# Unit 5 of every eight transposed by DMA instead of TensorE in a two-problem attention kernel

## The chip, the cores and the metric

The kernel runs on one core of one Trainium2 chip. The metric is the device time of one execution in microseconds, median of several runs.

## The reference

Two independent problems A and B of the same shape, outputs side by side. B repeats its keys `Hq // Hkv` = 1 times, so it is the same computation as A.

```python
B, Sq, D = 16, 144, 448
H, Sk, Dh = 16, 512, 256
q = (x @ wq).reshape(B, Sq, H, Dh).transpose(0, 2, 1, 3)
scores = einsum("bhqd,bhkd->bhqk", q, k_cache) * Dh ** -0.5
p = softmax(scores, axis=-1)
o = einsum("bhqk,bhkd->bhqd", p, v_cache)
out = o.transpose(0, 2, 1, 3).reshape(B, Sq, H * Dh) @ wo      # all bf16
```

## The kernel before

**Units.** A unit is one (problem, batch, head): 512 units in all (`NT`), 256 of A and then 256 of B. Eight units are a super-group (`SG`, 64 of them), four are a group (`G`). A unit has 144 query rows. 128 partitions don't hold them, so they are cut into `QA` = 112 rows, handled unit by unit, and a remainder of `QB` = 32 rows; the remainders of four units are stacked to one tile of 128 rows.

**Stages of a unit.**
- Q (`t_q`, L338): eight matmuls, x and Wq into one PSUM bank, moved to one of `NQT` = 12 slots of `qt_sb` by DVE or ACT (`t_evac_q`).
- SB (`t_sb`, L374): scores of the remainders of eight units at once, 16 matmuls at the first slot of a super-group; it is the first reader of the super-group's K. SA (`t_sa`, L471): scores of the 112 rows of one unit, two matmuls.
- Softmax of the 112 rows: maximum on DVE (L482), exponential with row sum on ACT into `pa_sb` (L493, `NPA` = 14 slots), reciprocal on DVE (L503), normalisation on POOL (`t_norm`, L511). The remainders do the same per group into `pb_sb` (L387, L397, L407, L415).
- P has its queries on partitions and must be transposed. The 112 rows: four TensorE transposes into PSUM (`t_ta`, L524) and a DVE copy into `pt_sb` (`t_evac_pta`, L534). The remainders: in the super-groups of `TB_SG` (0 to 7 and 28 to 37) TensorE (`t_tb`, L437) and DVE (L447); in the other 46 one transposing DMA per super-group, SBUF to SBUF, for both groups (`t_ptb_dma`, L425), from `pb_sb` into `pbt_sb`, which has one buffer (`NPBT` = 1). From `pbt_sb` POOL copies a group's remainders into `pt_sb` (`t_copy_ptb`, L457).
- PV (`t_pv`, L557): eight matmuls, moved to `ring` by ACT (L572, L574). OP (`t_op_piece`, L595): the output projection in pieces of two matmuls, spread over the slots; the result goes through `ost_sb` (`NOST` = 3 slots, L613) to the store (L624).

**Order.** The program is written out slot by slot; slot i is where unit i has its PV. In steady state SA and Q run ahead: SB of super-group n stands in slot 8n - 14, SA of unit u some 14 slots before its PV, TA (`LT`) two slots before it. Every engine executes its own list in order. `_Sched` adds the semaphore waits from the versions that each operation reads and writes; a write to a buffer waits for all readers of what it held.

**DMAs.** All are issued by SP, in one queue. `dma_plan` sorts them by a planned slot, and SP works the list off as fast as its waits let it; the planned slot sets the order only. K (`t_load_k`, L306) is 2 MB for a super-group, transposing, into one of `NK` = 2 buffers, so K of super-group n waits for the last SA of super-group n - 2. V (`t_load_v`, L316) is 1 MB for a group, five buffers. x (`t_load_x`, L296 and L297, transposing) serves two batches, 32 units. Wq (`t_load_wq`, L275 and L277) and Wo (L285) are loaded once for each problem, Wq in four quarters; B's replace A's around unit 256.

For each pair of super-groups n, n + 1 (n even, t = 8n) the list has this order (an x load stands first where (t + 32) is a multiple of 32):

```python
plan_x(t - 4, XG)
plan_pb(t - 4, n)          # the remainder's transposing DMA
plan_k(t - 3, n + 2)
plan_pb(t + 2, n + 1)
plan_k(t + 2, n + 3)
plan_v(t + 5 ...)          # three at t + 5, one at t + 8
```

and the quarters of B's Wq at `(4.9, 4.9, 8, 11)[hg] + NU - 32`, that is slots 228.9, 228.9, 232 and 235. The remainder's copies on POOL stand in slots 8n - 1 (first group) and 8n + 1 (second group).

Of the kernel before, what the change touches and what calls it, by code (L numbers as in the profile page):

```python
# [122 lines left out]
def bass_concat_heads__mha_block_cached__gqa_block_cached__near_ridge_kernel(  # L123
# [41 lines left out]
    TB_SG = set(range(RAMP)) | set(range(NSG // 2 - 4, NSG // 2 + 6))  # L165
    NK, NV, NXG = 2, 5, 2
# [5 lines left out]
    NQT, NPA, NPB, NPT, NST, NSTB, NOST = 12, 14, 2, 8, 4, 2, 3  # L172
# [9 lines left out]
    with contextlib.ExitStack() as es:  # L182
# [14 lines left out]
        pb_sb = sb("pb_sb", [128, NPB, 2, SK], BF16)  # L197
        pt_sb = sb("pt_sb", [128, NPT, 4, SQ], BF16)
        pbt_sb = sb("pbt_sb", [128, NPBT, 2, 4, 128], BF16)
# [38 lines left out]
        def t_ident():  # L238
            ones = pa_sb[:, 0, 0:128]

            def e1(g):
                return g.memset(ones, 1.0)
            S.add(POOL, e1, writes=[(("pa", 0), "ones")], name="ones")

            def e2(g):
                return g.affine_select(ident[:], ones, pattern=[[1, 128]], compare_op=ALU.is_equal,
                                       fill=0.0, base=0, channel_multiplier=-1)
            S.add(POOL, e2, reads=[(("pa", 0), "ones")], writes=[("ident", 0)], name="ident")

# [170 lines left out]
        def t_ptb_dma(SG):  # L420
            psl = SG % NPB
            tsl = SG % NPBT

            def e(q):
                return q.dma_start_transpose(pbt_sb[:, tsl, :, :, :].rearrange("p g c q -> p (g c) q"),  # L425
                                             pb_sb[:, psl, :, :].rearrange("p g k -> p (g k)")).then_inc(
                    sems["pb%d" % tsl], 16)
            S.add(SP, e, reads=[(("pb", psl, g), (2 * SG + g, 1)) for g in range(2)],
                  writes=[(("pbt", tsl, g), SG) for g in range(2)], dma_sem="pb%d" % tsl, name="pb%d" % SG)
# [56 lines left out]

        def t_exp(U):
            bank = U % 2
            sl = U % NST
            psl = U % NPA  # L490

            def e(a):
                return a.activation(pa_sb[0:QA, psl, :], sa_ps[bank][0:QA, :], AF.Exp,  # L493
                                    bias=stat[0:QA, NEG + sl:NEG + sl + 1], scale=1.0,
                                    accum_out=stat[0:QA, RSUM + sl:RSUM + sl + 1])
            S.add(ACT, e, reads=[(("sap", bank), ("s", U)), (("neg", sl), U)],
                  writes=[(("pa", psl), (U, 0)), (("rsum", sl), U)], banks=["sa%d" % bank], name="ex%d" % U)
# [8 lines left out]
        def t_norm(U):  # L506
            sl = U % NST
            psl = U % NPA

            def e(g):  # L510
                return g.tensor_tensor(pa_sb[0:QA, psl, :], pa_sb[0:QA, psl, :],  # L511
                                       stat[0:QA, RINV + sl:RINV + sl + 1].to_broadcast([QA, SK]), op=ALU.mult)
            S.add(POOL, e, reads=[(("pa", psl), (U, 0)), (("rinv", sl), U)], writes=[(("pa", psl), (U, 1))],
                  name="nm%d" % U)

        def t_ta(U):
            psl = U % NPA
# [114 lines left out]
        t_warm_zero()  # L632
        ta_bank = {}
        lag = [LAGS[min(n, len(LAGS) - 1)] for n in range(NSG)]
# [53 lines left out]
        for n in range(RAMP, NSG, 2):  # L688
            t = 8 * n
            XG = (t + 32) // (XB * H)  # L690
            if (t + 32) % (XB * H) == 0 and XG < NXGT:
                plan_x(t - 4, XG)
# [9 lines left out]
        for hg in range(HG):  # L702
            lo = q_slot[NU - H + 4 * hg + 3] + 1
            plan((4.9, 4.9, 8, 11)[hg] + NU - 32, lo, q_slot[NU + 4 * hg], t_load_wq, 1, hg)
# [35 lines left out]
        while True:  # L740
# [40 lines left out]
            if i % 8 == 1 and 0 <= i < NT:  # L781
                t_copy_ptb((i + 3) // 4)
            for u in sa_at.get(i - 1, ()):
# [3 lines left out]
            if 0 <= u < NT:  # L787
# [104 lines left out]
```

## Time and profile before

| | us |
|---|---|
| Time, median of 3 runs (lowest to highest) | 1221.61 (1216.64 to 1224.74) |
| The profiled execution's own time | 1215.54 |
| Its span, first to last instruction | 1213.8 |
| PE busy | 1171.0 (96%) |
| PE weight loads busy | 882.9 (73%) |
| ACT, DVE, POOL busy | 748.6, 743.7, 727.9 (60 to 62%) |
| Granted TensorE clock, mean | 0.992 |

How to read it. Times are microseconds unless marked ns. PE is TensorE's matmuls, PEld its weight loads; SPq is SP's queue, whose rows last from a DMA's issue until the queue is free for the next. A group's line has the source line, engine, operation, output and inputs, shapes and count, then busy time, mean ns of one, and the idle time of the engine just before them with what ended it. A row of the timeline has start, duration, engine, line, operation and count, and in brackets the idle time before it. A row of the table by stretches has the stretch, its length, busy time of each engine with its instructions, the granted clock, the share of the 16 DMA engines that packets held (it can pass 1, since packets overlap), and GB/s. Matmuls are pipelined, so the distance from one start to the next is a better measure of TensorE than the durations. Issuing instructions count as no engine's busy time.

### The profile page before, as it was taken

How to read it: one execution, taken by the hardware profiler on the slowest of the kernel's cores; microseconds unless marked ns; L12 is line 12 of the kernel's file. 1: busy time of each engine (PE TensorE's matmuls, PEld its weight loads, DVE VectorE, ACT ScalarE, POOL GpSimd, SP SyncE). 2: the span in 40 equal slices, each digit the busy share in tenths (PEclk: the TensorE clock that was granted, in tenths of full speed). 3: DMA queues.
4: the chain of work that ended last, by engine and by line, in shares of the span. 5: the costliest groups of instructions: out<-in, count | busy, mean ns of one | idle time of the engine just before them, and what ended most of it. 6: DMA issues, size and time to landing. Idle time of an engine off the chain costs nothing.

```text
span 1213.8 us, 33200 instructions
## 1 busy us (share of the span) xinstructions
PE 1171.0 (96%) x13612; PEld 882.9 (73%) x13612; DVE 743.7 (61%) x2088; ACT 748.6 (62%) x2213; POOL 727.9 (60%) x774
## 2 busy tenths in 40 slices
PE   6898999999999999999899989999999999999989
PEld 3676777777777777777577767777777777777766
DVE  3676666656656666666566656666666566566661
ACT  2565666666656666666566656666666666566662
POOL 1675576666566666666465656666666665665661
PEclk9998999999999999999899999999999999999999
DMA  9999999999999999999999899999999999899971
GB/s 244 281 264 293 286 266 194 249 264 271 262 286 194 266 253 279 271 260 247 296 231 268 252 258 255 269 279 251 266 237 242 255 285 284 224 247 249 245 208 56
DMA packets 679577, 306.18 MB, mean 252 GB/s; under 512 B 597504, under 2 KB 610304, under 8 KB 679424
## 3 DMA queue, kind: packets, MB, share of 16 engines
q1 hardware_dynamic: 679424, 304.05, 104.6%
q8 instruction: 107, 1.75, 0.6%
q14 instruction: 46, 0.38, 0.1%
HBM read 148.90 MB, written 4.13 MB: 126 GB/s over the span
## 4 chain that ended last, share of the span: by engine, by line
PE 80%; DMA 12%; DVE 3%; POOL 2%; SPq 1%; issue 1%; ACT 1%; DVEq 0%
PE ot_ps L557 17%; PE qp_ps L338 17%; PE sa_ps L471 16%; PE op_ps L595 16%; PE sa_ps L524 7%; DMA kt_sb<-in_A_k_cache_dram 6%; DMA kt_sb<-in_B_k_cache_dram 6%; PE sb_ps L374 5%; POOL pa_sb L511 1%; DVE stat L482 1%; SPq L306 1%; POOL pb_sb L415 1%; PE sb_ps L437 1%; ACT pa_sb L493 1%; PE qp_ps L595 1%
## 5 line engine op out<-in xcount | busy, mean ns | idle before, releaser
L511 POOL TENSOR_TENSOR pa_sb<-pa_sb,stat 112x512 bf16<-112x512 bf16 x512 | 532.3, 1041 | 458.2 <-DVE stat L503 432.7
L493 ACT ACTIVATE pa_sb<-sa_ps,stat 112x512 bf16<-112x512 f32 x512 | 352.6, 689 | 405.8 <-DVE stat L482 403.6
L482 DVE TENSOR_REDUCE stat<-sa_ps 112x1 f32<-112x512 f32 x512 | 354.0, 691 | 335.3 <-PE sa_ps L471 330.7
L338 PEld LDWEIGHTS qp_ps<-xt_sb,wq_sb 128*128 128x128 bf16 x4048 | 284.1, 98 | 81.6 <-DMA wq_sb<-in_A_wq_dram 3.9
L557 PE MATMUL ot_ps<-pt_sb,v_sb 128*128 128x144 bf16 x4096 | 341.8, 226 | 0.0
L338 PE MATMUL qp_ps<-xt_sb,wq_sb 128*128 128x144 bf16 x4048 | 337.4, 227 | 4.6 <-DMA wq_sb<-in_A_wq_dram 4.2
L471 PE MATMUL sa_ps<-kt_sb,qt_sb 128*112 128x512 bf16 x1024 | 314.0, 388 | 6.0 <-DVE pt_sb L534 5.2
L595 PE MATMUL op_ps<-wo_sb,ring 128*128 128x448 bf16 x1120 | 275.1, 353 | 0.0
L557 PEld LDWEIGHTS ot_ps<-pt_sb,v_sb 128*128 128x128 bf16 x4096 | 269.5, 98 | 0.4
L524 PEld LDWEIGHTS sa_ps<-ident,pa_sb 112*128 112x128 bf16 x2048 | 159.9, 114 | 113.6 <-ACT pa_sb L493 38.3
L534 DVE COPY pt_sb<-sa_ps 128x448 bf16<-128x448 bf16 x512 | 191.4, 374 | 19.9 <-PE sa_ps L524 19.9
L572 ACT ACTIVATE ring<-ot_ps 128x288 bf16<-128x288 f32 (+8 forms) x512 | 191.0, 373 | 19.4 <-PE ot_ps L557 19.2
L524 PE MATMUL sa_ps<-ident,pa_sb 112*128 112x112 bf16 x2048 | 187.3, 213 | 6.1 <-ACT pa_sb L493 6.1
L351 DVE TENSOR_SCALAR qt_sb<-qp_ps 128x288 bf16<-128x288 f32 x252 | 115.2, 457 | 95.0 <-PE qp_ps L338 94.1
L415 POOL TENSOR_TENSOR pb_sb<-pb_sb,stat 128x512 bf16<-128x512 bf16 x128 | 133.3, 1041 | 0.0
L471 PEld LDWEIGHTS sa_ps<-kt_sb,qt_sb 128*112 128x112 bf16 x1024 | 96.8, 130 | 46.0 <-issue 28.4
L355 ACT ACTIVATE qt_sb<-qp_ps 128x288 bf16<-128x288 f32 x254 | 105.5, 415 | 33.2 <-PE qp_ps L338 31.6
L595 PEld LDWEIGHTS op_ps<-wo_sb,ring 128*128 128x128 bf16 x1120 | 96.0, 98 | 31.8 <-ACT ring L572 0.2
L493 ACT ACTIVATION_READ_ACCUMULATOR pa_sb<-sa_ps,stat 112x1 f32 x512 | 99.4, 194 | 0.0
L397 ACT ACTIVATE pb_sb<-sb_ps,stat 128x512 bf16<-128x512 f32 x128 | 88.6, 692 | 0.8
L387 DVE TENSOR_REDUCE stat<-sb_ps 128x1 f32<-128x512 f32 x128 | 87.2, 681 | 0.0
L374 PE MATMUL sb_ps<-kt_sb,qt_sb 128*32 128x512 bf16 x1024 | 69.2, 391 | 18.2 <-DMA kt_sb<-in_B_k_cache_dram 11.3
(33 smaller groups left out, 353.6 us busy)
## 6 DMA issues: line engine op xcount, KB each, us to landing
v_sb<-in_A_v_cache_dram SPq DMA_DIRECT2D x64, 1024.0 KB, 8.9
v_sb<-in_B_v_cache_dram SPq DMA_DIRECT2D x64, 1024.0 KB, 8.9
out_dram<-ost_sb SPq DMA_DIRECT2D x36, 112.0 KB, 9.7
wo_sb<-in_A_wo_dram SPq DMA_DIRECT2D x8, 448.0 KB, 9.5
wo_sb<-in_B_wo_dram SPq DMA_DIRECT2D x8, 448.0 KB, 5.2
wq_sb<-in_A_wq_dram SPq DMA_DIRECT2D x4, 768.0 KB, 6.0
wq_sb<-in_B_wq_dram SPq DMA_DIRECT2D x4, 768.0 KB, 9.7
pbt_sb<-pb_sb SPq DMA_TRANSPOSE x46, 4.9
```

Of the source, the lines that this page charges most:

```text
L338: ins = t.matmul(acc[:, dc * SQ:(dc + 1) * SQ], lhsT=wq_sb[:, kc, c0:c0 + 128], rhs=xt_sb[:, xsl, kc, xo:xo + SQ], start=(kc == 0 and dc = ...
L374: ins = t.matmul(sb_ps[jj // 4][32 * j:32 * j + 32, :], lhsT=qt_sb[:, U % NQT, dc, QA:SQ], rhs=kt_sb[:, dc, (U % (8 * NK)) * SK:(U % (8 * ...
L415: return g.tensor_tensor(pb_sb[:, psl, G % 2, :], pb_sb[:, psl, G % 2, :], stat[:, RINVB + sl:RINVB + sl + 1].to_broadcast([128, SK]), op= ...
L471: ins = t.matmul(sa_ps[bank][0:QA, :], lhsT=qt_sb[:, U % NQT, dc, 0:QA], rhs=kt_sb[:, dc, ko:ko + SK], start=(dc == 0), stop=(dc == 1))
L482: return v.tensor_reduce(stat[0:QA, NEG + sl:NEG + sl + 1], sa_ps[bank][0:QA, :], axis=AX.X, op=ALU.max, negate=True)
L493: return a.activation(pa_sb[0:QA, psl, :], sa_ps[bank][0:QA, :], AF.Exp, bias=stat[0:QA, NEG + sl:NEG + sl + 1], scale=1.0, accum_out=stat ...
L511: return g.tensor_tensor(pa_sb[0:QA, psl, :], pa_sb[0:QA, psl, :], stat[0:QA, RINV + sl:RINV + sl + 1].to_broadcast([QA, SK]), op=ALU.mult)
L524: ins = t.transpose(pta_ps[bank][:, c * 128:c * 128 + QA], src[:, c, :], ident[0:QA, 0:QA])
L534: return v.tensor_copy(pt_sb[:, sl, :, 0:QA], pta_ps[bank][:, 0:512].rearrange("p (c q) -> p c q", c=4)[:, :, 0:QA])
L557: ins = t.matmul(ot_ps[ob][:, dc * SQ:(dc + 1) * SQ], lhsT=v_sb[:, vsl, j, c * DH + dc * 128:c * DH + (dc + 1) * 128], rhs=pt_sb[:, sl, c, ...
L572: ins = a.activation(ring[:, 2 * h:2 * h + 2, c0:c0 + n1], src[:, :, 0:n1], AF.Copy)
L595: ins = t.matmul(acc[0:m, 0:D], lhsT=ring[:, c, col0:col0 + m], rhs=wo_sb[:, c, :], start=(c == first), stop=(c == last))
```

## The change

P of unit 8n + 5, in the 46 super-groups whose remainders go through the DMA (`by_dma`), is written by ACT into a third slice of `pb_sb` instead of `pa_sb`, in the element order of the remainders, and is normalised there. The transposing DMA of the super-group takes three slices instead of two; it therefore also reads the normalised P of that unit. POOL copies the unit's 112 columns from `pbt_sb` into `pt_sb` (`t_copy_pta`, in slot 8n + 1, directly behind the second group's remainder). The unit's four TensorE transposes and its DVE copy fall away. Partitions 96 to 127 of the third slice are zeroed once at the start.

To make room: `NQT` 12 to 10, `NPA` 14 to 13 (with slots now counted over the units that use them), `NOST` 3 to 2. Two loads get other slots: the last quarter of B's Wq 240 instead of 235, which is behind K of super-group 32 (237) instead of ahead of it; x of group 10 slot 268 instead of 284, which is ahead of K of super-group 36 (269) instead of 38 (285).

```diff
--- before.py
+++ after.py
@@ -163,13 +163,15 @@
     LAGS = (7, 5, 6, 7, 8, 9, 10, 11, 12, 13, 14)
     RAMP = 8
     TB_SG = set(range(RAMP)) | set(range(NSG // 2 - 4, NSG // 2 + 6))
+    ADMA = (5,)
+    NPX = 2 + len(ADMA)
     NK, NV, NXG = 2, 5, 2
     WO_AT = ((12, 18, 26, 33), (277, 277, 293, 293))
     OP_FROM = (34, 34)
     N_WARM = (12, 16)
     XB = 2
     assert Bn % XB == 0
-    NQT, NPA, NPB, NPT, NST, NSTB, NOST = 12, 14, 2, 8, 4, 2, 3
+    NQT, NPA, NPB, NPT, NST, NSTB, NOST = 10, 13, 2, 8, 4, 2, 2
     NPBT = 1
     RS = 4
     RC = RS * 128
@@ -194,9 +196,9 @@
         xt_sb = sb("xt_sb", [128, NXG, 4, XB * SQ], BF16)
         qt_sb = sb("qt_sb", [128, NQT, 2, SQ], BF16)
         pa_sb = sb("pa_sb", [128, NPA, SK], BF16)
-        pb_sb = sb("pb_sb", [128, NPB, 2, SK], BF16)
+        pb_sb = sb("pb_sb", [128, NPB, NPX, SK], BF16)
         pt_sb = sb("pt_sb", [128, NPT, 4, SQ], BF16)
-        pbt_sb = sb("pbt_sb", [128, NPBT, 2, 4, 128], BF16)
+        pbt_sb = sb("pbt_sb", [128, NPBT, NPX, 4, 128], BF16)
         ost_sb = sb("ost_sb", [128, NOST, D], BF16)
         ident = sb("ident", [128, 128], BF16)
         stat = sb("stat", [128, 3 * NST + 3 * NSTB + 2], F32)
@@ -247,6 +249,11 @@
                                        fill=0.0, base=0, channel_multiplier=-1)
             S.add(POOL, e2, reads=[(("pa", 0), "ones")], writes=[("ident", 0)], name="ident")
 
+        def t_pb_zero():
+            def e(v):
+                return v.memset(pb_sb[96:128, :, 2:NPX, :], 0.0)
+            S.add(DVE, e, writes=[(("pb", psl, 2 + k), "z") for psl in range(NPB) for k in range(len(ADMA))], name="pbz")
+
         def t_warm_zero():
             def e(v):
                 return v.memset(pa_sb[:, 2:6, 0:128], 0.0)
@@ -425,8 +432,21 @@
                 return q.dma_start_transpose(pbt_sb[:, tsl, :, :, :].rearrange("p g c q -> p (g c) q"),
                                              pb_sb[:, psl, :, :].rearrange("p g k -> p (g k)")).then_inc(
                     sems["pb%d" % tsl], 16)
-            S.add(SP, e, reads=[(("pb", psl, g), (2 * SG + g, 1)) for g in range(2)],
-                  writes=[(("pbt", tsl, g), SG) for g in range(2)], dma_sem="pb%d" % tsl, name="pb%d" % SG)
+            S.add(SP, e, reads=[(("pb", psl, g), (2 * SG + g, 1)) for g in range(2)] +
+                  [(("pb", psl, 2 + k), ("a", 8 * SG + j, 1)) for k, j in enumerate(ADMA)],
+                  writes=[(("pbt", tsl, g), SG) for g in range(NPX)], dma_sem="pb%d" % tsl, name="pb%d" % SG)
+
+        def by_dma(U):
+            return U % 8 in ADMA and U // 8 not in TB_SG
+
+        def t_copy_pta(U):
+            SG = U // 8
+            tsl = SG % NPBT
+            k = 2 + ADMA.index(U % 8)
+
+            def e(g):
+                return g.tensor_copy(pt_sb[:, U % NPT, :, 0:QA], pbt_sb[:, tsl, k, :, 0:QA])
+            S.add(POOL, e, reads=[(("pbt", tsl, k), SG)], writes=[(("pta", U % NPT), U)], name="cpta%d" % U)
 
         def t_tb(G):
             psl = (G // 2) % NPB
@@ -484,17 +504,27 @@
             S.add(DVE, e, reads=[(("sap", bank), ("s", U))], writes=[(("neg", sl), U)], banks=["sa%d" % bank],
                   name="mx%d" % U)
 
+        def p_of(U):
+            if by_dma(U):
+                psl, k = (U // 8) % NPB, 2 + ADMA.index(U % 8)
+                return pb_sb[0:QA, psl, k, :], ("pb", psl, k), ("a", U)
+            psl = pa_slot[U]
+            return pa_sb[0:QA, psl, :], ("pa", psl), (U,)
+
         def t_exp(U):
             bank = U % 2
             sl = U % NST
-            psl = U % NPA
+            dst, key, ver = p_of(U)
 
             def e(a):
-                return a.activation(pa_sb[0:QA, psl, :], sa_ps[bank][0:QA, :], AF.Exp,
+                src = sa_ps[bank][0:QA, :]
+                if by_dma(U):
+                    src = src.rearrange("q (p c) -> q c p", c=4)
+                return a.activation(dst, src, AF.Exp,
                                     bias=stat[0:QA, NEG + sl:NEG + sl + 1], scale=1.0,
                                     accum_out=stat[0:QA, RSUM + sl:RSUM + sl + 1])
             S.add(ACT, e, reads=[(("sap", bank), ("s", U)), (("neg", sl), U)],
-                  writes=[(("pa", psl), (U, 0)), (("rsum", sl), U)], banks=["sa%d" % bank], name="ex%d" % U)
+                  writes=[(key, ver + (0,)), (("rsum", sl), U)], banks=["sa%d" % bank], name="ex%d" % U)
 
         def t_recip(U):
             sl = U % NST
@@ -505,16 +535,15 @@
 
         def t_norm(U):
             sl = U % NST
-            psl = U % NPA
+            dst, key, ver = p_of(U)
 
             def e(g):
-                return g.tensor_tensor(pa_sb[0:QA, psl, :], pa_sb[0:QA, psl, :],
-                                       stat[0:QA, RINV + sl:RINV + sl + 1].to_broadcast([QA, SK]), op=ALU.mult)
-            S.add(POOL, e, reads=[(("pa", psl), (U, 0)), (("rinv", sl), U)], writes=[(("pa", psl), (U, 1))],
-                  name="nm%d" % U)
+                return g.tensor_tensor(dst, dst, stat[0:QA, RINV + sl:RINV + sl + 1].to_broadcast([QA, SK]),
+                                       op=ALU.mult)
+            S.add(POOL, e, reads=[(key, ver + (0,)), (("rinv", sl), U)], writes=[(key, ver + (1,))], name="nm%d" % U)
 
         def t_ta(U):
-            psl = U % NPA
+            psl = pa_slot[U]
             bank = ta_bank[U]
 
             def e(t):
@@ -630,7 +659,12 @@
         t_wqzero()
         t_ident()
         t_warm_zero()
+        t_pb_zero()
         ta_bank = {}
+        pa_slot = {}
+        for u in range(NT):
+            if not by_dma(u):
+                pa_slot[u] = len(pa_slot) % NPA
         lag = [LAGS[min(n, len(LAGS) - 1)] for n in range(NSG)]
         sb_slot = [8 * n - lag[n] for n in range(NSG)] + [8 * NSG - lag[-1]]
         sa_slot = [sb_slot[u // 8] + (u % 8) * (sb_slot[u // 8 + 1] - sb_slot[u // 8]) // 8 for u in range(NT)]
@@ -689,7 +723,7 @@
             t = 8 * n
             XG = (t + 32) // (XB * H)
             if (t + 32) % (XB * H) == 0 and XG < NXGT:
-                plan_x(t - 4, XG)
+                plan_x(t - (20 if XG == 10 else 4), XG)
             plan_pb(t - 4, n)
             if n + 2 < NSG:
                 plan_k(t - 3, n + 2)
@@ -701,7 +735,7 @@
                     plan_v(t + at, 2 * n + 3 + j)
         for hg in range(HG):
             lo = q_slot[NU - H + 4 * hg + 3] + 1
-            plan((4.9, 4.9, 8, 11)[hg] + NU - 32, lo, q_slot[NU + 4 * hg], t_load_wq, 1, hg)
+            plan((4.9, 4.9, 8, 16)[hg] + NU - 32, lo, q_slot[NU + 4 * hg], t_load_wq, 1, hg)
         dma_plan.sort(key=lambda t: t[:2])
 
         u_tail0 = NT - H
@@ -780,11 +814,15 @@
                 t_copy_ptb((i + 1) // 4)
             if i % 8 == 1 and 0 <= i < NT:
                 t_copy_ptb((i + 3) // 4)
+            for k, j in enumerate(ADMA):
+                u = i + j - (1 if j > 2 else 0)
+                if (i - (1 if j > 2 else 0)) % 8 == 0 and 0 <= u < NT and by_dma(u):
+                    t_copy_pta(u)
             for u in sa_at.get(i - 1, ()):
                 t_recip(u)
                 t_norm(u)
             u = i + LT
-            if 0 <= u < NT:
+            if 0 <= u < NT and not by_dma(u):
                 ta_bank[u] = 1 - last_sa % 2 if sas else u % 2
                 t_ta(u)
                 t_evac_pta(u)
```

## The prediction

> **What bounds the kernel now.** I began with the summary of the page: who is busy, and what the chain that ended last is made of.
>
> ```profile
> PE 1171.0 (96%) x13612; PEld 882.9 (73%) x13612; DVE 743.7 (61%) x2088; ACT 748.6 (62%) x2213; POOL 727.9 (60%) x774
> DMA  9999999999999999999999899999999999899971
> PE 80%; DMA 12%; DVE 3%; POOL 2%; SPq 1%; issue 1%; ACT 1%; DVEq 0%
> ```
>
> TensorE carries 80% of the chain, and what interrupts it is DMA. DVE, ACT and POOL are 60% busy, so work on them costs only where someone waits for it. The groups by line name the work that the change touches, and the list of waits says which DMA stops TensorE:
>
> ```profile
> L524 PE MATMUL sa_ps<-ident,pa_sb 112*128 112x112 bf16 x2048 | 187.3, 213 | 6.1 <-ACT pa_sb L493 6.1
> L534 DVE COPY pt_sb<-sa_ps 128x448 bf16<-128x448 bf16 x512 | 191.4, 374 | 19.9 <-PE sa_ps L524 19.9
> L457 POOL COPY pt_sb<-pbt_sb 128x512 bf16<-128x512 bf16 x128 | 78.2, 611 | 10.9 <-PE ot_ps L557 10.9
> PE sb_ps L374 <- DMA kt_sb<-in_B_k_cache_dram: 11.3, 5, 5.3
> PE sb_ps L374 <- DMA kt_sb<-in_A_k_cache_dram: 6.5, 4, 3.2
> ```
>
> The only DMA that TensorE waits for once it runs is K, at line 374 (SB). How near the others are is read from the timeline of SP's queue. I write Kn for the K load of super-group n, pbn for its remainder's DMA. One pair of super-groups that has an x load, with the next pair's pb at its end (start, time on SP, line):
>
> ```profile
> 378.52 1.23 SPq L425 DMA_TRANSPOSE pbt_sb<-pb_sb  x1
> 379.80 9.47 SPq L306 DMA_TRANSPOSE kt_sb<-in_A_k_cache_dram  x1
> 389.32 3.75 SPq L316 DMA_DIRECT2D v_sb<-in_A_v_cache_dram  x4
> 396.69 4.20 SPq L296 DMA_TRANSPOSE xt_sb<-in_A_x_dram  x1
> 402.23 2.50 SPq L425 DMA_TRANSPOSE pbt_sb<-pb_sb  x1
> 404.77 8.39 SPq L306 DMA_TRANSPOSE kt_sb<-in_A_k_cache_dram  x1
> 414.53 1.23 SPq L425 DMA_TRANSPOSE pbt_sb<-pb_sb  x1
> ```
>
> pb19 starts at 378.52, when POOL's copy of the remainder before it (377.88 + 0.61) has freed the one pbt buffer. Then come K21, four V, x, pb20 and K22. K22 lands 10.5 us after 404.77, at 415.2, and SB 22 starts at 415.56. The table by stretches shows that nothing in between is spare:
>
> ```profile
> 376.00:379.00 3.00, 3.00 (x40) 2.44 (x38) 2.04 (x7) 1.58 (x5) 1.68 (x3) 1.00 0.00 0
> 387.00:389.50 2.50, 2.50 (x31) 1.94 (x29) 1.73 (x6) 2.24 (x9) 1.53 (x3) 1.00 1.27 290
> 394.00:401.00 7.00, 7.00 (x88) 5.03 (x86) 3.77 (x11) 4.60 (x13) 3.68 (x4) 1.00 1.02 383
> 379.70:415.20 35.50, 35.50 (x420) 27.36 (x413) 22.79 (x64) 22.36 (x65) 22.23 (x25) 1.00 1.13 267
> 1184.50:1185.90 1.40, 1.40 (x9) 0.76 (x8) 0.00 (x0) 0.00 (x0) 1.03 (x2) 1.00 1.04 190
> ```
>
> Last two columns: share of the 16 DMA engines, GB/s. Before pb19 they stand still (0.00); from its first packet until K22 lands they are never free (1.13). So each pair has a DMA chain, from the odd pb's issue to the even K's landing, which must fit into TensorE's time from the same moment to that SB. Read off in this way for all pairs with two pb in the chain, taking TensorE's time without the wait:
>
> - Nine pairs with an x load (K14, 18, 22, 26, 42, 46, 50, 54, 58): DMA 36.3 to 38.0 us, mean 37.22; TensorE mean 37.18. They are level; waits of 2.5 us in all.
> - Eleven without (K12, 16, 20, 24, 28, 44, 48, 52, 56, 60, 62): DMA mean 35.05, TensorE mean 37.41. Slack of 2.4 us, except K16 (0.3) and K60 (short by 1.1, and waited for so long).
>
> **The change, part by part.** It holds for 46 super-groups (64 less the 18 of TB_SG).
>
> Removed from TensorE: four transposes each. From the start of a unit's L524 to the start of its L557 the timeline has 0.20 us (413.88 to 414.08; median over the trace 0.199). 46 x 0.20 = -9.2 us where TensorE sets the pace; 0.40 a pair. The 46 copies at L534 leave DVE, which is off the path: nothing. The exponential reads PSUM in the order of the remainder's (L397 692 ns, L493 689): nothing.
>
> Added on POOL: 46 copies 128x448. L457 moves 128x512 in 611 ns, so 448/512 x 611 = 0.53 us, 0.55 with its start. As work this is hidden: the normalisation behind it on POOL is used by TensorE some eleven units later. (Uncovered it would be 46 x 0.55 = 25 us.) As a wait it is not: the copy frees pbt directly after the remainder's second copy, and the odd pb, with the odd K behind it on SP, stands waiting for just that. So each chain starts 0.55 us later. Late next is the even K.
>
> Added to DMA: a third slice, 512 packets of 256 bytes, in each of 46 transposes. pb63 runs alone: 1024 packets in the 1.4 us from 1184.5, at 190 GB/s mean with its ends, so 131 KB takes 0.60 to 0.69. On SP itself nothing: pb's 1.23 us for 1024 packets is what x takes for 288 (L297, 1.24). For the even pb, in a full queue, I take 0.6. For the odd one I take 0.5: it starts on an idle queue, and K's packets ramp up slowly behind it, so part may hide. Bounds for a slice: 0 from below, hidden in that ramp; from above 1.0, half of what a pb adds to a K (odd pb's issue to K's landing about 13.0, K37 with no pb 11.4, K35 10.6, so about 2.0). The chain grows by 0.55 + 0.5 + 0.6 = 1.65 us; ends 0.55 and 2.55.
>
> [...]
>
> Sum over the pairs. With x: DMA 37.22 + 1.65 = 38.87; TensorE 37.18 - 0.40 = 36.78; a wait of 2.09 in place of 0.28, nine times, +16.3. Without x: the chain becomes 36.7, and TensorE's time is 37.0 plus the 2 us that the pair before has just waited (the next chain starts at the odd pb, just ahead of that wait): no new wait; K60 about as before. So +16.3 - 9.2 = +7.1 us.
>
> Moved: two loads in the middle, each taken out from in front of a K that TensorE waits for.
>
> ```profile
> 574.55 2.64 SPq L275 DMA_DIRECT2D wq_sb<-in_B_wq_dram  x1
> 579.85 0.55 SPq L275 DMA_DIRECT2D wq_sb<-in_B_wq_dram  x1
> 601.26 1.04 PE L374 MATMUL sb_ps<-kt_sb,qt_sb 128*32 128x512 bf16 x8 [5.28 <-DMA kt_sb<-in_B_k_cache_dram]
> 713.84 1.54 PE L374 MATMUL sb_ps<-kt_sb,qt_sb 128*32 128x512 bf16 x16 [3.38 <-DMA kt_sb<-in_B_k_cache_dram]
> ```
>
> Wq's last quarter (both its DMAs, at 579.85 and 580.45) goes behind K32. The quarter before it has landed at 589.35 and this one at 592.1, so K32 comes 2.5 us sooner: the wait of 5.28 becomes 2.8. Its new place, ahead of K33, has 11 us of slack, and Q of unit 268 needs it some four units after SB 32, about 9 us. The x load of group 10 (two DMAs) goes from in front of K38 to in front of K36. An x costs 37.22 - 35.05 = 2.2 us in a chain: SB 38 waits 1.2 instead of 3.38. K36 has 5.9 us of slack and keeps 3.7. K30, with one three-slice pb in its chain, falls some 0.7 us short, but SB 32's wait, counted from K31, takes that up. Together -4.7; bounds 0 (something else holds these K) and -8.7 (both waits gone).
>
> Fewer buffers: ten Q slots still hold the unit before last, whose SA is behind TensorE when the evacuation comes; thirteen P slots are read one unit before they are written; two output slots leave 15.6 us between a store's landing and the next use at the tightest. Nothing, all three. The zeroing at the start (L252's like took 0.27 us, on DVE) lies under the first loads.
>
> Total +7.1 - 4.7 = +2.4 us. The profiled execution took 1215.5, its span 1213.8 and 1.7 around it; it would become 1217.9. It lies 6.1 below the median of the runs shown, so I forecast that median with the same difference: 1224.0.
>
> **Rivals.** *Third slice and copy are hidden* (faster). For it: K's ramp after an odd pb ran at 109 GB/s for 1.7 us, so there is room. Against: in the x pairs the queue is full at the even pb. Then 9.2 and 4.7 are both won: 1207.7.
>
> *The third slice is dear* (slower): the even pb in the full queue costs far more than its packets, and the x pairs' K come later by all of it. For it: pb20 took 6.1 us to land, and half of that for half as much again would be 3.0; pb19, on an idle queue, took 4.2, half 2.1. The chain would grow by 5.65, nine waits become 6.1, net 52.4 - 9.2 - 4.7: 1260. It passes +1% from a growth of 2.75 us on. Against: most of those 6 us are spent behind x and V.
>
> *The moved loads bring nothing*: 1228.7, still within 1%.
>
> **How the numbers follow.** Forecast 0.6, hidden 0.15, dear 0.2, moves in vain 0.05. The forecast's own ends: growth 0.55 makes the x pairs wait 1.0 each, and -2.8 - 4.7 in all; growth 2.55 gives 24.4 - 9.2 - 4.7 = +10.5. So 1214 to 1232; with the runs' spread of some 4 us and part of both rivals 1208 to 1238. One per cent, 12 us, is about what a measurement of this kernel can tell from no change: faster 0.14, same 0.65, slower 0.21.
>
> **What would show it.** L524 with 1864 matmuls; a new POOL copy of about 0.53 us; the odd pb released by it, 0.55 us after the remainder's copy; pb still 1.2 us on SP; SB waits of about 2 us at K14, 18, 22 and their like, none at the others; SB 32 and SB 38 waiting 2 to 4 us less. Wrong if the x pairs show no new waits (hidden), or if pairs without x wait too (dear).

## The result and the profile after

The changed kernel took 1222.42 us in the median of its runs, from 1213.26 to 1227.86; the kernel before, on the same chip, 1216.71. The ratio is 1.0038, with a 95% interval of 1.0019 to 1.0056: 0.4% slower, against the 0.2% (1224.0 us from 1221.61) that was predicted. A later comparison of the same two kernels (e10 below) gave 1.0064 [1.0042, 1.0086], which lies wholly above the forecast 1.002. The profiled execution of the changed kernel took 1227.86 us, its span 1226.0; it lies at the upper end of that kernel's runs, so its 12.2 us over the span before (1213.8) are about twice what the medians differ by. The second comparison left another profile, with a span of 1223.8; I use it where one execution could mislead.

The page first, engines and the shares of the chain:

```profile
PE 1168.1 (95%) x13428; PEld 876.8 (72%) x13428; DVE 730.5 (60%) x2043; ACT 745.8 (61%) x2213; POOL 748.3 (61%) x820
PE 70%; DMA 21%; DVE 3%; ACT 2%; SPq 1%; POOL 1%; issue 1%; DVEq 0%
```

TensorE has 184 matmuls less (46 x 4) and is busy 2.9 us less; its idle time (span less busy) went from 42.8 to 57.9 us, +15.1. These two make the 12.2. DMA's share of the chain went from 12% to 21%. POOL has 46 instructions more. The groups by line have the removed and the added work, and the list of waits has the price:

```profile
L563 DVE COPY pt_sb<-sa_ps 128x448 bf16<-128x448 bf16 x466 | 173.4, 372 | 20.6 <-PE sa_ps L553 20.6
L553 PE MATMUL sa_ps<-ident,pa_sb 112*128 112x112 bf16 x1864 | 170.9, 214 | 6.8 <-ACT pa_sb L523 6.8
L448 POOL COPY pt_sb<-pbt_sb 128x448 bf16<-128x448 bf16 x46 | 25.8, 560 | 0.0
PE sb_ps L381 <- DMA kt_sb<-in_B_k_cache_dram: 17.2, 9, 3.1
PE sb_ps L381 <- DMA kt_sb<-in_A_k_cache_dram: 14.9, 9, 3.7
```

L553 is the former L524, L563 the former L534, L381 the former L374 (SB). The two waits for K were 17.8 us together in nine places; they are 32.1 in eighteen. The pair whose SP queue the prediction showed looks like this now. POOL's two copies ahead of the odd pb come first (the line above them is the one copy of before), then SP's queue:

```profile
377.88 0.61 POOL L457 COPY pt_sb<-pbt_sb 128x512 bf16<-128x512 bf16 x1
```

```profile
379.12 0.61 POOL L477 COPY pt_sb<-pbt_sb 128x512 bf16<-128x512 bf16 x1
379.67 0.56 POOL L448 COPY pt_sb<-pbt_sb 128x448 bf16<-128x448 bf16 x1
```

```profile
380.26 1.40 SPq L432 DMA_TRANSPOSE pbt_sb<-pb_sb  x1
381.70 8.35 SPq L313 DMA_TRANSPOSE kt_sb<-in_A_k_cache_dram  x1
390.10 4.01 SPq L323 DMA_DIRECT2D v_sb<-in_A_v_cache_dram  x4
397.72 4.90 SPq L303 DMA_TRANSPOSE xt_sb<-in_A_x_dram  x1
403.95 3.37 SPq L432 DMA_TRANSPOSE pbt_sb<-pb_sb  x1
407.36 10.01 SPq L313 DMA_TRANSPOSE kt_sb<-in_A_k_cache_dram  x1
417.42 1.36 SPq L432 DMA_TRANSPOSE pbt_sb<-pb_sb  x1
```

Before, pb19 was issued 0.03 us after the second remainder copy had ended. Now the new copy stands between them, and pb19 is issued 0.03 us after the end of that one; it is so in all nine x pairs. K22 landed at 419.46, and TensorE, in its timeline, stood still for 3.06 us for it, where it had waited for nothing (the first line is SB 22 before, with no bracket; a bracket is the idle time before the instruction and what ended it):

```profile
415.56 0.82 PE L374 MATMUL sb_ps<-kt_sb,qt_sb 128*32 128x512 bf16 x9
```

```profile
419.51 1.05 PE L381 MATMUL sb_ps<-kt_sb,qt_sb 128*32 128x512 bf16 x16 [3.06 <-DMA kt_sb<-in_A_k_cache_dram]
606.29 1.05 PE L381 MATMUL sb_ps<-kt_sb,qt_sb 128*32 128x512 bf16 x16 [2.31 <-DMA kt_sb<-in_B_k_cache_dram]
644.20 1.05 PE L381 MATMUL sb_ps<-kt_sb,qt_sb 128*32 128x512 bf16 x16 [1.68 <-DMA kt_sb<-in_B_k_cache_dram]
718.38 1.05 PE L381 MATMUL sb_ps<-kt_sb,qt_sb 128*32 128x512 bf16 x8 [2.96 <-DMA kt_sb<-in_B_k_cache_dram]
```

The last three lines are SB 32 (it was 5.28), SB 34 (new) and SB 38 (it was 3.38). The stretches of the same pair show the queue as full as before:

```profile
377.00:381.00 4.00, 4.00 (x52) 3.13 (x53) 2.40 (x7) 2.44 (x8) 3.03 (x5) 1.00 0.55 125
381.50:419.40 37.90, 34.95 (x408) 26.82 (x400) 22.18 (x62) 22.87 (x67) 23.68 (x26) 1.00 1.15 261
411.50:413.30 1.80, 1.80 (x24) 1.44 (x22) 1.27 (x5) 1.08 (x3) 1.05 (x2) 1.00 1.26 58
420.50:423.80 3.30, 3.30 (x21) 2.19 (x18) 1.65 (x4) 1.45 (x5) 1.04 (x1) 0.50 1.14 213
424.00:427.30 3.30, 3.30 (x41) 2.59 (x39) 1.53 (x5) 1.52 (x7) 1.25 (x2) 1.00 1.29 293
```

The DMA engines are free before the odd pb (0.55 over those 4 us, the end of the work before) and busy from its first packet until K22 has landed (1.15). The last three lines are for the section on the hardware.

The table has, for every run, the DMA chain C and TensorE's time P as the prediction defines them, the mean over the nine pairs with an x load and over the eleven without, and the sums of the SB waits in them. P is counted from the issue of the odd pb, so the copy ahead of it shows as a shorter P and not as a longer C. "Busy" and "idle" are TensorE's in the profiled span. Each ratio is to the kernel before, run beside it. All columns behind the ratio come from one profiled execution, which need not be a typical one: e1's was the second longest of its twelve, e6's the shortest of its nine.

| kernel | ratio to before [95%] | span | busy, idle | x pairs: C, P, waits | others: C, P, waits | SB 32, 34, 38 |
|---|---|---|---|---|---|---|
| before | 1 | 1213.8 | 1171.0, 42.8 | 37.22, 37.18, 2.5 | 35.05, 37.41, 1.2 | 5.3, 0, 3.4 |
| after | 1.0038 [1.0019, 1.0056] | 1226.0 | 1168.1, 57.9 | 38.41, 36.50, 17.6 | 36.61, 38.17, 1.9 | 2.3, 1.7, 3.0 |
| e10 (after again) | 1.0064 [1.0042, 1.0086] | 1223.8 | 1163.1, 60.7 | 38.27, 36.58, 16.2 | 36.48, 37.82, 3.7 | 3.8, 0, 3.0 |
| e1 moves only | 0.9948 [0.9926, 0.9971] | 1215.6 | 1170.2, 45.4 | 37.66, 37.18, 6.2 | 35.67, 37.75, 0.0 | 3.3, 0, 2.5 |
| e2 no moves | 1.0075 [1.0043, 1.0107] | 1224.3 | 1161.6, 62.7 | 38.15, 36.53, 15.4 | 36.73, 37.65, 3.1 | 4.7, 0, 4.3 |
| e3 copy early | 0.9982 [0.9956, 1.0008] | 1215.2 | 1163.4, 51.8 | 38.24, 37.07, 11.5 | 36.45, 38.10, 3.4 | 2.2, 0.2, 3.6 |
| e4 x in the gap | 0.9998 [0.9975, 1.0021] | 1220.9 | 1163.1, 57.8 | 37.25, 36.14, 11.7 | 36.99, 37.67, 5.9 | 2.7, 0, 3.4 |
| e5 saving alone | 0.9901 [0.9866, 0.9936] | 1209.2 | 1161.8, 47.4 | 37.61, 37.09, 5.5 | 35.69, 37.43, 2.6 | 2.2, 0, 3.4 |
| e6 moves, x in the gap | 0.9924 [0.9895, 0.9953] | 1207.1 | 1165.8, 41.3 | 35.52, 36.95, 1.8 | 35.86, 37.29, 0.9 | 3.0, 1.7, 1.9 |
| e7 after, e3 and e4 | 0.9947 [0.9924, 0.9970] | 1212.5 | 1163.4, 49.1 | 36.83, 36.60, 5.9 | 36.92, 37.39, 4.5 | 3.8, 0, 2.9 |
| e8 slice alone | 1.0022 [0.9993, 1.0051] | 1225.3 | 1175.0, 50.3 | 38.08, 37.68, 8.2 | 36.71, 38.32, 4.8 | 2.9, 0, 2.3 |
| e9 waits filled | 1.0068 [1.0043, 1.0092] | 1223.6 | 1170.0, 53.6 | 38.57, 37.75, 8.4 | 36.40, 37.91, 2.8 | 1.7, 2.6, 2.7 |

### The profile page after: what moved, and what is told of

Read it like the earlier page. It is cut to its first block, busy times and chain, and to the rows that moved or that the text cites. A ratio compares the mean times of both kernels' runs of the same rounds, so it can differ in the third digit from the quotient of the medians.

```text
span 1226.0 us, 32835 instructions
## 1 busy us (share of the span) xinstructions
PE 1168.1 (95%) x13428; PEld 876.8 (72%) x13428; DVE 730.5 (60%) x2043; ACT 745.8 (61%) x2213; POOL 748.3 (61%) x820
## 4 chain that ended last, share of the span: by engine, by line
PE 70%; DMA 21%; DVE 3%; ACT 2%; SPq 1%; POOL 1%; issue 1%; DVEq 0%
PE ot_ps L586 15%; PE qp_ps L345 15%; PE op_ps L624 15%; PE sa_ps L491 14%; DMA kt_sb<-in_B_k_cache_dram 11%; DMA kt_sb<-in_A_k_cache_dram 9%; PE sa_ps L553 6%; PE sb_ps L381 5%; DVE stat L502 1%; SPq L313 1%; POOL pa_sb L541 1%; ACT pa_sb L523 1%; DVE qt_sb L358 1%; PE qp_ps L624 0%; PE sb_ps L457 0%
## 5 line engine op out<-in xcount | busy, mean ns | idle before, releaser
L541 POOL TENSOR_TENSOR pa_sb<-pa_sb,stat 112x512 bf16<-112x512 bf16 x466 | 483.8, 1040 | 403.2 <-DVE stat L533 321.8
L523 ACT ACTIVATE pa_sb<-sa_ps,stat 112x512 bf16<-112x512 f32 x466 | 320.3, 687 | 375.9 <-DVE stat L502 374.7
L586 PEld LDWEIGHTS ot_ps<-pt_sb,v_sb 128*128 128x128 bf16 x4096 | 272.9, 98 | 10.1 <-POOL pt_sb L477 0.4
L553 PEld LDWEIGHTS sa_ps<-ident,pa_sb 112*128 112x128 bf16 x1864 | 144.4, 114 | 107.3 <-ACT pa_sb L523 38.8
L563 DVE COPY pt_sb<-sa_ps 128x448 bf16<-128x448 bf16 x466 | 173.4, 372 | 20.6 <-PE sa_ps L553 20.6
L553 PE MATMUL sa_ps<-ident,pa_sb 112*128 112x112 bf16 x1864 | 170.9, 214 | 6.8 <-ACT pa_sb L523 6.8
L381 PE MATMUL sb_ps<-kt_sb,qt_sb 128*32 128x512 bf16 x1024 | 69.1, 391 | 32.3 <-DMA kt_sb<-in_B_k_cache_dram 17.2
L523 ACT ACTIVATION_READ_ACCUMULATOR pa_sb<-sa_ps,stat 112x1 f32 x466 | 90.2, 194 | 0.0
```

The lines of the kernel that those rows point to most:

```text
L381: ins = t.matmul(sb_ps[jj // 4][32 * j:32 * j + 32, :], lhsT=qt_sb[:, U % NQT, dc, QA:SQ], rhs=kt_sb[:, dc, (U % (8 * NK)) * SK:(U % (8 * ...
L523: return a.activation(dst, src, AF.Exp, bias=stat[0:QA, NEG + sl:NEG + sl + 1], scale=1.0, accum_out=stat[0:QA, RSUM + sl:RSUM + sl + 1])
L541: return g.tensor_tensor(dst, dst, stat[0:QA, RINV + sl:RINV + sl + 1].to_broadcast([QA, SK]), op=ALU.mult)
L553: ins = t.transpose(pta_ps[bank][:, c * 128:c * 128 + QA], src[:, c, :], ident[0:QA, 0:QA])
L563: return v.tensor_copy(pt_sb[:, sl, :, 0:QA], pta_ps[bank][:, 0:512].rearrange("p (c q) -> p c q", c=4)[:, :, 0:QA])
L586: ins = t.matmul(ot_ps[ob][:, dc * SQ:(dc + 1) * SQ], lhsT=v_sb[:, vsl, j, c * DH + dc * 128:c * DH + (dc + 1) * 128], rhs=pt_sb[:, sl, c, ...
```

## The experiments

The theory under test is the prediction's: three terms, a TensorE saving, a longer DMA chain (slice and copy) that turns into waits in the x pairs, and a gain from two moved loads. A price read from the difference of two ratios has an uncertainty of some 0.003 to 0.004 (the half widths of the two intervals, added as squares), 4 to 5 us. The two comparisons of the changed kernel, after and e10, themselves lie 3.2 us apart, so a price read from the changed kernel is given beside both.

**e1, the moves alone, and e2, all but the moves.** e1 is the kernel before with these two lines of the change; e2 is the changed kernel with both undone.

```
-                plan_x(t - 4, XG)
+                plan_x(t - (20 if XG == 10 else 4), XG)
...
-            plan((4.9, 4.9, 8, 11)[hg] + NU - 32, ...
+            plan((4.9, 4.9, 8, 16)[hg] + NU - 32, ...
```

> The kernel before with nothing but the two moved loads (x of group 10 to slot 268, Wq's last quarter to slot 240). Chain theory: the waits at SB 32 (5.28 us) and SB 38 (3.38) fall to 2 to 3 us each, a wait of up to 1.7 us may come at SB 34, whose K now stands behind that quarter; 2 to 6 us under the kernel before, 1211 to 1215 beside its 1216.7. The x pairs stay level: their waits stay at about 2.5 us in all. Rival, the moves only shift the waits: no difference, 1216.7.

> The changed kernel with both loads back in their old slots: the third slice alone. Chain theory: 2 to 6 us over the changed kernel, 1224 to 1228, 8 to 11 us over the kernel before; x pairs wait 1.5 to 2.5 us each as in the changed kernel. Rival, the moves cost and the slice is free: at or under the changed kernel's 1222.4.

e1 gave 0.9948, that is -6.3 us [-9.0, -3.5]: the moves bring something, and the rival "moves in vain" falls. Undoing them in e2 raised the ratio from 1.0038 to 1.0075, +4.5 us with an uncertainty of some 4.5 (+1.3 beside e10), which agrees, but would not show it alone. The profile of e1 shows where: SB 32 waits 3.3 instead of 5.3 and SB 38 2.5 instead of 3.4. That is 2.9 us, less than the ratio; the profile itself has x pairs with 3.7 us more of waits than the profile before, though nothing in them was edited. One profile's waits scatter that much, and the mean C with them: it is 0.44 us longer in the x pairs and 0.62 in the others. The ratio shows more than the profile's waits explain: in the profile before, TensorE ran at half clock for 6.8 us around SB 32 (from 598.2 on), in e1's for 3.4, which would be another 1.7 us at most, since 3.1 of the 6.8 us lie in the wait itself; the rest is open.

**e3, the copy out of the chain.** In the changed kernel POOL does the new copy before the remainder's second copy and not after it:

```
-                u = i + j - (1 if j > 2 else 0)
-                if (i - (1 if j > 2 else 0)) % 8 == 0 and 0 <= u < NT and by_dma(u):
+                u = i + j
+                if i % 8 == 0 and 0 <= u < NT and by_dma(u):
                     t_copy_pta(u)
```

> The changed kernel, with POOL's copy of unit 5 one slot earlier, ahead of the second remainder's copy, so that the odd transposing DMA no longer waits 0.56 us for it. Chain theory: the chain of each x pair starts 0.56 us sooner, its wait falls from about 2.0 to 1.4 us; nine times 0.56 is 5 us, more if waits near 3 us also cost TensorE clock: 1212 to 1217.5. Rival, the chain hangs on something else than that copy: 1222, as the changed kernel.

The ratio fell to 0.9982 [0.9956, 1.0008]: -6.8 us against the 1.0038 of the changed kernel. POOL's timeline shows the order, SP's the odd pb right behind the remainder's copy:

```profile
373.33 0.56 POOL L448 COPY pt_sb<-pbt_sb 128x448 bf16<-128x448 bf16 x1
375.34 0.61 POOL L477 COPY pt_sb<-pbt_sb 128x512 bf16<-128x512 bf16 x1
```

```profile
375.98 1.39 SPq L432 DMA_TRANSPOSE pbt_sb<-pb_sb  x1
```

In the x pairs C stayed (38.24 against 38.41), P grew from 36.50 to 37.07, by 0.57, close to the 560 ns of the copy, and the waits fell from 17.6 to 11.5. In all nine the odd pb is now issued 0.03 us after the remainder's copy. Nine times 0.56 is 5.0 us; 6.8 were measured, with some 4 of uncertainty (10.0 beside e10). So as a wait the copy costs about its own duration for each x pair, as the prediction had it. That it is hidden as work fits: all 46 copies are still in e3, which is no slower than the kernel before, where 25 us of uncovered work would show.

**e4, x loads where the queue was thought to be free.** Each x load of the steady part goes behind the even K of the pair before.

```
-                plan_x(t - (20 if XG == 10 else 4), XG)
+                plan_x(t - (18 if XG > 3 else 4), XG)
```

> The changed kernel, with every x load from group 4 on issued right behind the even K of the pair before, just ahead of the odd transposing DMA, where the DMA engines stood still for about 2 to 3 us. Chain theory: the x pairs' DMA time falls by the 1.8 to 2.2 us of an x, from 38.4 to about 36.4, level with TensorE's 36.5; 17.6 us of waits become 2 to 5, and time that follows from them in the TensorE clock goes too: 1201 to 1209, under both kernels. Rival, an x costs the same in any chain (it holds up the odd transposing DMA and the chain that starts with it): 1222, with waits in other pairs.

The ratio became 0.9998 [0.9975, 1.0021], 4.9 us under the changed kernel, where I had expected 13 to 21. SP's queue, from K24's issue on:

```profile
445.20 10.00 SPq L313 DMA_TRANSPOSE kt_sb<-in_A_k_cache_dram  x1
455.24 1.29 SPq L303 DMA_TRANSPOSE xt_sb<-in_A_x_dram  x1
456.58 1.25 SPq L304 DMA_TRANSPOSE xt_sb<-in_A_x_dram  x1
457.87 1.48 SPq L432 DMA_TRANSPOSE pbt_sb<-pb_sb  x1
```

Here the odd pb follows x at once: x has held it up. That is so in three of the nine places (pb15, pb23 and pb47); in the other six POOL's copy still releases the pb, 0.1 to 3.0 us after x's issue is over. In seven of the nine, x lands 0.5 to 3.9 us after the odd pb's issue, so the chain behind shares the DMA engines with it. C of the x pairs fell by 1.16 and not by the 1.8 to 2.2 of a whole x; that of the others rose by 0.38, and their waits from 1.9 to 5.9 (3.7 in e10, so little of this is clear of the scatter). The load is hidden in part. Neither expectation was met: the rival had the waits of other pairs, but not the gain.

**e5, the saving alone.** In the changed kernel the third slice and the copy are left out: P of unit 5 is not transposed in the 46 super-groups, and PV reads an earlier unit's P there.

```
-  ... pbt_sb[:, tsl, :, :, :] ... pb_sb[:, psl, :, :]
+  ... pbt_sb[:, tsl, 0:2, :, :] ... pb_sb[:, psl, 0:2, :]
...
-                    t_copy_pta(u)
+                    pass
...
+            W = U
+            while by_dma(W):
+                W -= 8
-  reads=[(("v", vsl), G), (("pta", sl), U), ...
+  reads=[(("v", vsl), G), (("pta", sl), W), ...
```

> The changed kernel without the third slice and without POOL's copy of unit 5, so that P of unit 5 is not transposed at all in the 46 super-groups (its PV reads the P of an earlier unit that lies in the slot): TensorE's saving with neither of its prices, the moves included. Chain theory: DMA chains as in the kernel before, 37.2 to 37.7 us with x and 35.0 to 35.7 without, TensorE 0.4 us shorter; x pairs wait 0.5 to 1.2 us each, so some 4 to 6 of the 9.2 us remain on top of the moves' 6: ratio to the kernel before 0.985 to 0.992. Rival, TensorE's saving is not worth its 0.20 us a unit: as the moves alone, 0.995.

0.9901 [0.9866, 0.9936], and 0.0047 under e1, which keeps the transposes (and the larger buffers): 5.7 us with an uncertainty of some 5, where 9.2 is the work removed. TensorE is busy 8.4 us less than in e1 (1170.2 to 1161.8), and idle 2.0 us more (45.4 to 47.4). The saving on the engine is about the predicted one. That part of it becomes a wait in the x pairs, because C and P are level there, is not shown: their waits are 5.5 us here and 6.2 in e1's profile, and the 2.6 new ones are in the other pairs.

**e6 and e7, the two placements without and with the slice.** e6 is the kernel before with Wq's quarter moved and the x loads as in e4; e7 is the changed kernel with the edits of e3 and e4.

> The kernel before with the moved Wq quarter and with every x load from group 4 on right behind the even K of the pair before (no third slice). In the changed kernel that move gave nothing, because there the DMA engines had no gap left: its chains of both kinds, 38.4 and 36.6 us, came to more than TensorE's two times 36.5. Here the chains are 37.2 and 35.0 against 37.2 and 37.4. Theory of a full queue: a gap is left, the x pairs' waits (2.5 to 6 us in all) go, and with them little else: ratio 0.990 to 0.995. Rival, x costs the same wherever it stands: as the moves alone, 0.995, or worse.

> The changed kernel with POOL's copy one slot earlier and the x loads right behind the even K of the pair before, both. Chain theory with a full queue: the early copy takes 0.56 us from each chain, x in the gap 0.4 us from the mean chain; ratio to the kernel before 0.993 to 0.999. Rival (the gains of the two are the same gain): 0.998, as with the early copy alone.

e6: 0.9924 [0.9895, 0.9953]. e7: 0.9947 [0.9924, 0.9970]. Both beat the kernel before. In e6, at the same place as in e4's lines, the x load falls into a gap:

```profile
435.03 10.68 SPq L306 DMA_TRANSPOSE kt_sb<-in_A_k_cache_dram  x1
445.75 1.29 SPq L296 DMA_TRANSPOSE xt_sb<-in_A_x_dram  x1
447.08 1.24 SPq L297 DMA_TRANSPOSE xt_sb<-in_A_x_dram  x1
449.15 1.24 SPq L425 DMA_TRANSPOSE pbt_sb<-pb_sb  x1
```

Here the odd pb comes 0.83 us after the end of x's issue, so the queue still had room there. One place does not tell the two kernels apart, though: in e6 too, three of the nine odd pb (15, 39 and 43) follow x at once, and x lands behind the odd pb's issue in eight. What differs is how full the queue is: C of the two kinds of pairs adds up to 71.4 us in e6, against 74.2 of P, and to 74.2 in e4, against 73.8. C of the x pairs went from 37.22 to 35.52 and that of the others only from 35.05 to 35.86; all twenty pairs together wait 2.7 us. SB 22 starts without a wait, in TensorE's timeline:

```profile
414.10 1.05 PE L374 MATMUL sb_ps<-kt_sb,qt_sb 128*32 128x512 bf16 x16
```

With the slice (e7) the two kinds of pairs wait 10.4 us. Two pairs of runs ask whether the slice pays once its copy is out of the chain: e7 lies 0.0023 over e6, and e3 0.0034 over e1, each with an uncertainty of some 0.0036. So no gain of the slice is shown at any placement tried, and no clear loss either. e6 is the version to keep: it beats both kernels with two lines changed (from e1 it is not told apart).

**e8, the slice alone.** e1 with a third slice of zeros in each of the 46 transposes, which nobody reads; TensorE keeps all its transposes and POOL gets no copy. The buffers are those of the changed kernel. The main lines:

```
+    NPX = 3
...
-    NQT, NPA, NPB, NPT, NST, NSTB, NOST = 12, 14, 2, 8, 4, 2, 3
+    NQT, NPA, NPB, NPT, NST, NSTB, NOST = 10, 13, 2, 8, 4, 2, 2
...
-        pb_sb = sb("pb_sb", [128, NPB, 2, SK], BF16)
+        pb_sb = sb("pb_sb", [128, NPB, NPX, SK], BF16)
...
-        pbt_sb = sb("pbt_sb", [128, NPBT, 2, 4, 128], BF16)
+        pbt_sb = sb("pbt_sb", [128, NPBT, NPX, 4, 128], BF16)
```

> The kernel before with the two moved loads, and a third slice that holds zeros in each of the 46 transposing DMAs, used by nobody: unit 5 stays on TensorE, POOL copies nothing more, nothing waits longer. The price of 512 packets alone. Chain theory: chains 1.1 us longer (0.5 odd, 0.6 even), 38.3 and 36.2, TensorE unchanged at 37.2; x pairs wait 1.1 us more each, 8 to 10 us over the moves alone: ratio to the kernel before 1.000 to 1.005. Rival, the slice is free: 0.995. Rival, it is dear: over 1.01.

1.0022 [0.9993, 1.0051], against 0.9948 for e1: +9.0 us with an uncertainty of some 4.5, 0.20 us for each slice. C grew by 0.42 in the x pairs (37.66 to 38.08) and by 1.04 in the others (35.67 to 36.71), where 1.1 had been the term for both slices of a pair. The table settles this better than one pair of profiles: C of the other pairs is 35.05 to 35.86 in the four kernels without the slice and 36.40 to 36.99 in the eight with it, 1.1 us apart in the mean; C of the x pairs, where x keeps its place, 37.2 to 37.7 in three and 38.1 to 38.6 in six, 0.8 apart. The smaller buffers are not the reason: e5 has them, without the slice, and lies with the short chains (37.61 and 35.69). What they cost in time was not tested alone. So the rival "hidden" falls.

Where the 9.0 us arise is less clear. I had expected them in the x pairs; in e8's profile these wait only 2.0 us more than in e1's, the others 4.8 more, and TensorE is busy 4.8 us longer. Half the length of each stretch at half clock counts as lost (in the profile after, 3.3 us at 0.50 have 21 matmuls, the same length at 1.00 has 41), and that is 11.9 us in e8's profile and 6.8 in e1's, so by this count most of the longer busy time is the clock. The groups by line confirm that TensorE kept its work:

```profile
L530 PE MATMUL sa_ps<-ident,pa_sb 112*128 112x112 bf16 x2048 | 187.3, 213 | 5.1 <-ACT pa_sb L499 5.0
```

**e9, the waits filled, and e10, the changed kernel beside it.** TensorE's clock fell to half behind many of the waits: over all twelve traces, behind 49 of 64 idle times of 1.95 us or more. To separate the wait from what the clock does behind it, e9 puts twenty matmuls that nobody needs (identity by identity, into a bank that SB overwrites; `t_fill`, not shown) ahead of SB in the nine x pairs.

```
+                    if u // 8 in (14, 18, 22, 26, 42, 46, 50, 54, 58):
+                        t_fill(u // 8)
```

> The changed kernel with 20 small matmuls (identity by identity, about 1.1 us of TensorE, result overwritten) just ahead of SB in the nine x pairs, where TensorE waits for K anyway. In the profiles so far every TensorE idle time of 3.0 us or more was followed by about 3.4 us at a granted clock of 0.5, those from 2.0 to 3.0 us about every second time, none below 1.9. Clock theory: the idle times of the x pairs become about 1 us instead of 2, K lands as before, and the four half-clock stretches behind them (1.7 us each) go: 3 to 7 us under the changed kernel on the same chip, for work added. Rival, the wait itself is all and the clock follows something else: equal to the changed kernel, or up to 9 us over it where the filler finds no wait.

> The changed kernel once more, to stand beside the filler on the same chip: ratio to the kernel before 1.002 to 1.006 as on record; half-clock stretches behind the idle times over 2 us of its x pairs.

The groups by line and the timeline of TensorE have the filler:

```profile
L378 PE MATMUL sb_ps<-ident 128*128 128x128 bf16 x180 | 11.5, 219 | 0.0
```

```profile
416.04 1.28 PE L378 MATMUL sb_ps<-ident 128*128 128x128 bf16 x20
419.50 1.90 PE L389 MATMUL sb_ps<-kt_sb,qt_sb 128*32 128x512 bf16 x16 [2.18 <-DMA kt_sb<-in_A_k_cache_dram]
```

The waits of the x pairs fell from 16.2 us (e10) to 8.4, by less than the 11.5 us of filler; the time lost at half clock fell from 8.5 to 6.8 us. The ratios are the same, 1.0068 and 1.0064. The expected gain did not come, and behind the wait of 2.18 us that stood after the filler, in the line above, SB itself took 1.90 us instead of 1.05, as at half clock. So e9 decides nothing about the clock's share, which stays open. What it does show is that 11.5 us of work, most of it put into waits, did not move the ratio by more than its uncertainty (some 4 us).

## Why the prediction came out as it did

The terms, as ratios and in us, beside the prediction. Its +16.3 for the nine x pairs is taken apart into what each part adds to C or takes from P (1.1 slices, 0.55 copy, 0.40 TensorE), and the 0.24 by which the waits of before are more than the difference of their mean C and P:

| term | from | measured | predicted |
|---|---|---|---|
| moves | e1 to before | -0.0052, -6.3 | -4.7 (0 to -8.7) |
| TensorE saving | e5 to e1 | -0.0047, -5.7 | -9.2 + 9 x 0.40 = -5.6 |
| third slice | e8 to e1 | +0.0074, +9.0 | 9 x 1.1 = +9.9 |
| copy in the chain | after to e3 | +0.0056, +6.8 | 9 x 0.55 = +5.0 |
| slack counted | | | 9 x (0.04 - 0.28) = -2.2 |
| sum | | +0.0031, +3.8 | +2.4 |
| all of it | after to before | +0.0038, +4.6 (e10: +0.0064) | +2.4 |

The measured terms carry 3 to 5 us of uncertainty each and their sum some 7. Each has the predicted sign; that the sum comes within 1 us of the whole is in part luck.

**The chain of the x pairs: right.** Waits of 1.96 us each were measured (1.80 in e10), 2.09 predicted. With the copy counted into P, the prediction has C 38.3 and P 36.23; the profile has 38.41 and 36.50. The other pairs have no new wait of weight: 1.9 us in all, 1.2 before. Their P grew to 38.17; the prediction's 37.0 + 2, less 0.55 for the copy, is 38.4.

**The copy: right.** 560 ns instead of 0.53 us, on the path of the odd pb. **SP: right where the queue has room.** The shortest pb there takes 1.27 us beside 1.23; the median of the 46, full queue included, went from 1.47 to 1.90.

**The moves: right in sum, wrong in their parts.** SB 32 came to 2.3 us where 2.8 was predicted (the two landings that the prediction reads, 589.35 and 592.1, are 2.75 us apart and not 2.5). SB 38 came to 3.0 where 1.2 was. The step that failed is "An x costs 37.22 - 35.05 = 2.2 us in a chain": K38's chain, counted from K37's issue, shrank only from 39.44 to 39.0 in the changed kernel, and SB 38's wait fell by 0.4 there and by 0.9 in e1. A mean difference between two kinds of pairs was used as the price of one load in one place. SB 34's wait of 1.68 us was not foreseen at all: "its new place, ahead of K33, has 11 us of slack" is true of K33, but K34 stands behind it. SP's timeline in the middle:

```profile
587.83 16.27 SPq L313 DMA_TRANSPOSE kt_sb<-in_B_k_cache_dram  x1
604.15 0.58 SPq L282 DMA_DIRECT2D wq_sb<-in_B_wq_dram  x1
604.77 0.49 SPq L284 DMA_DIRECT2D wq_sb<-in_B_wq_dram  x1
605.31 12.25 SPq L313 DMA_TRANSPOSE kt_sb<-in_B_k_cache_dram  x1
...
623.48 3.69 SPq L303 DMA_TRANSPOSE xt_sb<-in_B_x_dram  x1
627.21 3.33 SPq L304 DMA_TRANSPOSE xt_sb<-in_B_x_dram  x1
630.59 18.30 SPq L313 DMA_TRANSPOSE kt_sb<-in_B_k_cache_dram  x2
```

K33, behind the quarter of Wq, landed 15.86 us after its issue; the x load and K34 follow in the same queue. The wait is not in every profile (0.2 in e3, none in e1 or e10, 1.7 in e6, 2.6 in e9), so it is at the edge; that the slack of the chain behind K33 counted, and not K33's, fits the times and was not tested. With SB 34 the waits at the moved loads fell by 1.7 us in the changed kernel and by 2.9 in e1, where the ratio gives 6.3: that the sum of -4.7 comes close is luck in part.

**TensorE's saving: right in size; what the level pairs take back is not shown.** Of 9.2 us of work the prediction let 3.6 turn into waits in the x pairs; e5 took 8.4 us of busy time off e1 and 5.7 of the time, but with an uncertainty of some 5 us, and without new waits in the x pairs.

**What the sum left out.** The busy time of the changed kernel fell by 2.9 us and not by 9.2. Its profile lost 15.4 us at half clock, the one before 10.2, which makes up 5.2 of the 6.3. This belongs to the execution as much as to the change: e10, the same kernel, lost 8.5 and was busy 1163.1; by 9.2 less work and 1.7 less at half clock it should have been 1160.1, so 3 us of busy time are open there. Of the 15.1 us of new idle time, 15.1 are in the x pairs, +0.7 in the others, -3.0 in SB 32, -0.4 in SB 38 and +1.7 in SB 34, which makes 14.1; 1 us of idle time and, in this profile, 1 us of busy time are open.

**The rivals.** "Hidden" is refuted by e8 (9.0 us more, and longer chains wherever the slice is) and e3 (the copy costs 6.8). "The third slice is dear" needs C to grow by 5.65 with the copy in it, or 2.75 to pass 1%; it grew by 1.19 in the x pairs, 1.75 with the copy's 0.56. "Moves in vain" is refuted by e1.

## What to carry to other kernels

Where an engine and a DMA queue are level within each period, do not count on a gain from moving work from one to the other; here none was shown even after the queue had been given some slack (e7 beside e6). Compare the chain and the engine's time period by period, and count from the event that releases the chain, with every small copy that stands ahead of it. Where a load stands in the queue was worth more here (e6, 0.9924, two lines) than what the work was done on. When a load is moved, follow the slack of everything queued behind its new place, not only of the next transfer.

## What the hardware showed that I had not expected

**TensorE's clock often falls after idle times of 2 us.** In the profile after, SB 22's wait of 3.06 us is followed by 3.4 us at a granted clock of 0.50, of which the stretch from 420.50 above shows 3.3, with 21 matmuls; the same length right after it, at 1.00, has 41 (the stretch from 424.00). Where TensorE has work for all of it, such a stretch loses 1.7 us, half its length. Over the twelve traces, from 30 us on, I compared each idle time of TensorE with the clock behind it: of 59 between 1.0 and 1.95 us none was followed by a stretch at half clock, of 38 between 1.95 and 3.0 us 24 were, and of 26 of 3.0 us or more 25 were. So from 3.0 us on a fall was all but certain in these traces, and from 1.95 us on it was already likelier than not. As an estimate from these numbers, a wait of 2 us can cost nearly 4 (2 + 1.7). What of this reaches the end of the kernel e9 did not settle.

**The transposing DMA all but stands still for some 1.1 us at a time.** The stretch from 411.50 above is one place: all engines hold packets (1.26) and move 58 GB/s (8 GB/s in the 1.45 us from 411.85 on), where 261 is the mean of the pair. I counted some 45 such stretches of at least 0.75 us in the profile before (50 us in all, 1.1 each) and some 49 after (53 us, 1.1 each); the count moves by a few with where a stretch is cut off. 39 of the 45, and 39 of the 49, begin within 1.6 us after a packet of the queue that carries instructions, of which there are some 105:

```profile
q8 instruction: 105, 1.72, 0.6%
```

By chance it would be about 14% (105 times 1.6 us of 1226). That one causes the other was not tested. One or two of them more or fewer in a chain are as large as the scatter of C from pair to pair (37.4 to 39.3 over the nine x pairs after), which may be part of why a single profile's waits differ by several us between executions of one kernel.
